# Spacing the weight, x and g tiles apart in SBUF, with one temporary slot fewer

## The chip, the cores and the metric

The kernel runs on one core of a Trainium2 chip. The metric is the device time of one execution in microseconds (us). Beside the timed executions there is one execution taken by the hardware profiler, and every view of the profile shown below is of that one.

## The reference

The program is an attention over a narrow band of scores, followed by a gated feed-forward layer, all in float32. Cut to what is computed:

```python
# q, k, v: (8 batches, 8 heads, 576, 64); tau = 0.02
scores = q @ k.T / sqrt(64)
scores = where(scores >= max(scores) - tau, scores, -1e9)   # row-wise maximum
attn = exp(scores - max(scores)); attn /= attn.sum() + 1e-9
x = (attn @ v)  # -> 4608 tokens x 512
gate = 1 / (1 + exp(-(x @ w_gate)))   # w_gate, w_val: 512 x 1536
val = x @ w_val
out = (gate * val) @ w_out            # w_out: 1536 x 512
```

## The kernel before, in words

**Numbers in two parts.** TensorE works in a single-pass float32 form (`F32R`), so an operand that has to be precise is split into a high part and a low part, and a product takes three matmuls (high·high, high·low, low·high). A tile with two parts is written as `[P, 2, 512]`: 4096 bytes in each of the 128 partitions.

**Two streams of work.** The attention goes through visits: one batch and one pair of heads, batch after batch. Each visit loads k, q and v, splits them, and goes through score tiles of 128 queries: scores `s` on TensorE (PE, L559), the maximum (DVE, L566), the threshold (L571 or L575), the exponential (ACT, L580), the masking with the row sums (DVE, L583), the normalisation (POOL, L613), transposes `tp` and `lk` (PE, L628, L657, L666) with their copies (L635, L638, L645, L672, L675), and the product with v, `av` (PE, L716 or L729), gathered in `xf` and split into an `x` tile (L738, L740). Batch 0 (`PLAIN`) uses plain float32 matmuls, four passes instead of the split.

The feed-forward part (called moe) goes through blocks of 512 tokens, eight from the batches and a ninth from the 64 left-over tokens of each batch. A block has `in_units`: for each of the 12 slices f of d_ff, 12 matmuls for the gate and 12 for the value, `m` (L781), then tanh into a temporary `th` (ACT, L791), the gated product (DVE, L795), and its split into a `g` tile (ACT L799, POOL L801). Then `out_units`: 4 output tiles of 36 matmuls each, `o` (L817), copied (ACT, L827) into a temporary `ot` and stored. Block 0 comes in two halves of 256 tokens. The weights are split once, in 36 conversions (L389 to L428, each with a temporary `wa`), written to DRAM and streamed back into `w` tiles for every later block (`wi` at L760 for m, `wo` for o).

**Tiles in memory.** All tiles of a tag rotate through a fixed number of slots (`SLOTS`): 7 of `w` (raw weights, split weights, streamed weights), 5 of `x`, 12 of `g` (and, early on, split weights `ws`), and 5 of `t2`, the 2048-byte temporaries: `wa` in a conversion, `th` from tanh to POOL's split, `avt` (L732) between two halves of `av`, and `ot`. Each w, x and g slot is 4096 bytes, so that all slots of these three tags begin at the same remainder of 512 bytes: in the built program it is 32 for each of them. The operands of one matmul start at multiples of 512 bytes within them. The operands of `s` and `av` start at multiples of 128 bytes within their tiles, which also begin at 32 past a multiple of 512 (or 288, for one of the `pl` slots). A tile `pad` of 224 bytes (`PAD = 56` floats) lies ahead of all.

**What sets the order.** The kernel issues nothing directly: every operation is recorded with its engine, an assumed cost and a key. `Plan.run` then goes through a list schedule with one free or busy flag for each engine; of the ready operations it takes the one with the smallest key whose tiles find room in `SLOTS`. moe matmuls have the lowest priority on PE (keys from 1e6), so they fill what the attention leaves. The order found this way is the program's order on each engine; on the chip each engine works through its own list and waits on semaphores. The number of `t2` slots thus counts twice: in the order, and on the chip, where a tile's next user waits for the last reader of the slot.

Of the kernel before, what the change touches and what calls it, by code (L numbers as in the profile page):

```python
# [2 lines left out]

# [39 lines left out]
class Plan:  # L43
# [12 lines left out]

    def make(self, b):
        pool, bufs = self.pools[b.tag]
        return pool.tile(b.shape, b.dtype, tag=b.tag, name=b.name, bufs=bufs)

    def op(self, eng, cost, key, emit, reads=(), writes=(), also=(), leave=0, behind=None, after=(), lag=0.0):

# [136 lines left out]
SLOTS = {  # L199
    "kn": 1, "qn": 1, "vn": 1, "k2": 1, "q2": 1, "kd": 3, "qd": 3, "vs": 2,  # L200
    "p": 3, "pc": 1, "sm": 8, "st": 8, "pt": 2, "pl": 2, "ptc": 1, "plc": 1, "xf": 2, "x": 5, "g": 12,
    "w": 7, "t2": 5,
}
PHASES = True
LEAD = 5
# [20 lines left out]
PE_UNTIL, POOL_UNTIL = 36, 72  # L226
AHEAD = 5

PAD = 56


def act(n):
# [16 lines left out]
def kernel(  # L249
# [48 lines left out]

    cp.tile([P, PAD], F32, tag="pad", name="pad")
    ident = cp.tile([P, P], F32, tag="ident", name="ident")  # L300
# [690 lines left out]
```

## Time and profile before

| | |
|---|---|
| median of 2 timed runs | 1477.87 us (1477.44 to 1478.29) |
| the profiled execution's own time | 1478.33 us |
| its span, first to last instruction | 1476.4 us |
| granted TensorE clock, mean | 0.986 |
| busy in the span: PE, DVE, ACT, POOL | 1428.2, 962.6, 792.5, 655.1 us |
| HBM traffic over the span | 172 GB/s |

The span leaves out 1.9 us of the profiled execution's time. PE is TensorE's matmuls and PEld its weight loads, one ahead of each matmul, which run beside the matmul before. A matmul's recorded duration (some 390 ns for 512 columns) is its latency; successive matmuls overlap, so that their pace is read from a group's time over its count in an undisturbed stretch. A row of the chain of waits gives the start, the length and the line of each piece of work that the end hung on, with the count of instructions in it. A row of the table by stretches gives each engine's busy time with its count in brackets, then the granted clock.

### The profile page before, as it was taken

Reading aid. Unit: us, or ns where it says so; the run is one execution under the profiler, and the core shown is the slowest. Engines: PE = TensorE matmul, PEld = TensorE weight load, DVE = VectorE, ACT = ScalarE, POOL = GpSimd, SP = SyncE. Lnnn points to the kernel's source line nnn. Section 1 sums busy time; section 2 is a strip of 40 time slices with the busy share of each in tenths; the row PEclk is TensorE's granted clock in tenths of the full one; section 3 lists DMA queues with packets and bytes.
Section 4 is the critical chain, followed back from the end, with each engine's and each line's share of the span. In section 5 each row is a group of like instructions: output and inputs, shape, how many; then the busy total and the mean of one; then the engine's idle time right before and its main releaser. Section 6 shows DMA issues by size and latency. Waiting matters only on the chain.

```text
span 1476.4 us, 23618 instructions
## 1 busy us (share of the span) xinstructions
PE 1428.2 (97%) x7960; PEld 1222.8 (83%) x7960; DVE 962.6 (65%) x2064; ACT 792.5 (54%) x1674; POOL 655.1 (44%) x766
## 2 busy tenths in 40 slices
PE   7899878899999999999999999999999999999998
PEld 4588778788888888888888888988888888888887
DVE  6888888888865897388918993789558852010010
ACT  6677656567645675376627663666456743121120
POOL 5668665654644355244533454444434442122120
PEclk9999979899999999999999999999999999999999
DMA  7877979686775658666666677557847454756663
GB/s 262 288 241 235 291 238 269 184 263 178 195 232 179 198 177 260 193 188 206 191 215 186 184 210 259 144 171 211 276 143 201 144 186 147 247 199 205 214 195 120
DMA packets 116551, 307.22 MB, mean 208 GB/s; under 512 B 17104, under 2 KB 38096, under 8 KB 116432
## 3 DMA queue, kind: packets, MB, share of 16 engines
q1 hardware_dynamic: 116432, 305.71, 67.1%
q8 instruction: 65, 1.06, 0.3%
q14 instruction: 54, 0.44, 0.1%
HBM read 224.92 MB, written 29.36 MB: 172 GB/s over the span
## 4 chain that ended last, share of the span: by engine, by line
PE 80%; DVE 8%; POOL 3%; ACT 3%; issue 2%; DMA 2%; SPq 0%; POOLq 0%; DVEq 0%; ACTq 0%
PE m L781 36%; PE o L817 17%; PE s L559 7%; PE av L729 7%; PE tp L628 5%; DVE p L583 2%; PE s_l L559 1%; DVE pt L645 1%; DVE st L566 1%; DVE sm L608 1%; POOL p L613 1%; DVE pl L675 1%; PE tp_l L628 1%; PE lk L666 1%; ACT p L580 1%
## 5 line engine op out<-in xcount | busy, mean ns | idle before, releaser
L781 PE MATMUL m<-x,wi 128*128 128x512 f32 x2016 | 495.7, 395 | 0.5 <-DMA wi<-wid 0.5
L781 PEld LDWEIGHTS m<-x,wi 128*128 128x128 f32 x2016 | 366.6, 188 | 69.2 <-issue 0.9
L817 PE MATMUL o<-g,wo 128*128 128x512 f32 x1296 | 343.7, 402 | 0.0
L613 POOL TENSOR_SCALAR p<-p,w_t,sm 128x576 f32<-128x576 f32 x224 | 188.2, 850 | 234.0 <-DVE sm L611 226.3
L795 DVE SCALAR_TENSOR_TENSOR th<-th,m 128x512 f32<-128x512 f32 (+1 forms) x120 | 75.8, 631 | 326.4 <-PE m L781 325.0
L801 POOL TENSOR_TENSOR g<-th,g 128x512 fp32r<-128x512 f32 (+1 forms) x120 | 141.6, 1180 | 307.7 <-ACT g L799 307.2
L817 PEld LDWEIGHTS o<-g,wo 128*128 128x128 f32 x1296 | 228.2, 189 | 37.9
L583 DVE SCALAR_TENSOR_TENSOR p<-s,st,p 128x576 f32<-128x576 f32 x224 | 181.2, 812 | 24.9 <-ACT p L580 17.8
L559 PE MATMUL s<-kd,qd 128*128 128x288 f32 x896 | 162.2, 305 | 13.1 <-DVE p L583 8.9
L580 ACT ACTIVATE p<-s,st 128x576 f32<-128x576 f32 x224 | 164.7, 737 | 13.3 <-DVE st L566 12.4
L799 ACT CAST g<-th 128x512 fp32r<-128x512 f32 (+1 forms) x120 | 69.1, 576 | 190.3 <-DVE th L795 190.3
L645 DVE TENSOR_TENSOR pt<-tp,pt 128x512 fp32r<-128x512 f32 x224 | 151.5, 687 | 25.4 <-ACT pt L638 19.2
L566 DVE TENSOR_REDUCE st<-s 128x1 f32<-128x576 f32 x224 | 163.4, 750 | 6.8 <-PE s L559 3.6
L559 PEld LDWEIGHTS s<-kd,qd 128*128 128x128 f32 x896 | 138.5, 191 | 35.4 <-DVE p L583 12.5
L638 ACT CAST pt<-tp 128x512 fp32r<-128x512 f32 x224 | 129.0, 587 | 49.1 <-PE tp L628 46.3
L729 PE MATMUL av<-pt,vs 128*128 128x320 f32 (+1 forms) x896 | 142.1, 302 | 1.0 <-DVE pt L645 0.6
L729 PEld LDWEIGHTS av<-pt,vs 128*128 128x128 f32 x896 | 133.7, 195 | 9.2 <-DVE pt L645 0.8
L628 PE MATMUL tp<-ident,p 128*128 128x128 f32 x896 | 131.8, 274 | 1.3 <-POOL p L613 1.0
L628 PEld LDWEIGHTS tp<-ident,p 128*128 128x128 f32 x896 | 108.3, 141 | 13.7 <-POOL p L613 4.5
L791 ACT ACTIVATE th<-m 128x512 f32<-128x512 f32 (+1 forms) x120 | 66.8, 556 | 96.4 <-POOL g L801 47.9
L571 ACT ACTIVATE st<-st,ntau_t 128x1 f32<-128x1 f32 x192 | 56.6, 295 | 92.3 <-DVE st L566 90.6
L733 DVE TENSOR_TENSOR xf<-av,avt 64x256 f32<-64x256 f32 x112 | 50.8, 454 | 37.3 <-ACT avt L732 36.1
(345 smaller groups left out, 1791.6 us busy)
## 6 DMA issues: line engine op xcount, KB each, us to landing
wi<-wid SPq DMA_DIRECT2D x192, 512.0 KB, 5.9
wo<-wod SPq DMA_DIRECT2D x108, 512.0 KB, 4.7
kd<-k SPq DMA_DIRECT2D x112, 320.0 KB, 5.3
qd<-q SPq DMA_DIRECT2D x112, 128.0 KB, 4.7
wid<-ws SPq DMA_DIRECT2D x24, 512.0 KB, 5.1
out_dram<-ot SPq DMA_DIRECT2D x36, 256.0 KB, 2.2
kn<-in_k_dram SPq DMA_DIRECT2D x28, 320.0 KB, 4.2
qn<-in_q_dram SPq DMA_DIRECT2D x28, 320.0 KB, 6.0
```

What stands on the lines that cost most here:

```text
L559: nc.tensor.matmul(s.ap[:, c, :HALF], st(), mv(slice(k0 + c * HALF, k0 + (c + 1) * HALF)), start=m == 0, stop=m == len(steps) - 1,)
L566: op("DVE", 0.76, key, lambda: nc.vector.tensor_reduce(out=st.ap[:, 0:1], in_=sv(), axis=AX.XY, op=ALU.max, negate=True), reads=[s], write ...
L580: op("ACT", 0.74, key, lambda: nc.scalar.activation(p(), sv(), AF.Exp, bias=st.ap[:, 0:1], scale=1.0), reads=[s, (st, 0)], writes=[(g.p, i)])
L583: op("DVE", 0.9, key, lambda: nc.vector.scalar_tensor_tensor(out=p(), in0=sv(), scalar=st.ap[:, 1:2], in1=p(), op0=ALU.is_ge, op1=ALU.mult ...
L613: op("POOL", 0.9, key, lambda i=i: nc.gpsimd.tensor_scalar(out=p.ap[:, i * S : (i + 1) * S], in0=p.ap[:, i * S : (i + 1) * S], scalar1=w_t ...
L628: nc.tensor.matmul(tp.ap[:, c, :], self.p.ap[:, o + c * P : o + (c + 1) * P], ident, is_transpose=True, start=c == 0, stop=c == NJ - 1, sk ...
L638: op("ACT", 0.58, key, lambda: nc.scalar.copy(hi(), tp.ap), reads=[tp], writes=[(self.pt, (0, i))])
L645: op("DVE", 0.69, key, lambda: nc.vector.tensor_tensor(out=lo(), in0=tp.ap, in1=f32(hi()), op=ALU.subtract), reads=[tp, (self.pt, (0, i))] ...
L729: nc.tensor.matmul(av.ap, st, mv, start=i == 0, stop=i == len(ms) - 1)
L781: nc.tensor.matmul(m.ap, wv[:, a, c * P : (c + 1) * P], xs[c].ap[:, z, c0:c1], start=e == 0, stop=e == 11,)
L801: op("POOL", pool(W), -1, lambda th=th, hi=hi, f=f: nc.gpsimd.tensor_tensor(out=g[f].ap[:, 1, c0:c1], in0=th.ap, in1=f32(hi()), op=ALU.sub ...
L817: nc.tensor.matmul(acc.ap, wv[:, f, a], g[fg * ND + f].ap[:, z], start=(fg, f, a, z) == (0, 0, 0, 0), stop=(fg, f, a, z) == (NFG - 1, ND - ...
```

## The change

Each w tile is allocated 8 floats longer than it is, each x and g tile 24 floats longer, and only the first part is used; the tile that the kernel sees has the shape and the contiguous layout that it had. The slots then lie 4128 bytes (w) and 4192 bytes (x, g) apart, so that in the built program the seven w slots begin at remainders of 512 of 384, 416, 448, 480, 0, 32 and 64, and the seventeen g and x slots take each multiple of 32 at least once. The room for this (1856 bytes) comes from `t2`, which has four slots instead of five, and from `PAD`. `PAD` also moves everything that lies ahead of the w tiles by 160 bytes: kd, qd and vs now begin at remainder 384, and the pt tiles, which lie behind them, at 96.

```diff
     def make(self, b):
         pool, bufs = self.pools[b.tag]
-        return pool.tile(b.shape, b.dtype, tag=b.tag, name=b.name, bufs=bufs)
+        if b.tag not in STAGGER:
+            return pool.tile(b.shape, b.dtype, tag=b.tag, name=b.name, bufs=bufs)
+        n = math.prod(b.shape[1:])
+        t = pool.tile([b.shape[0], n + STAGGER[b.tag]], b.dtype, tag=b.tag, name=b.name, bufs=bufs)
+        if len(b.shape) == 2:
+            return t[:, :n]
+        names = "abc"[: len(b.shape) - 1]
+        return t[:, :n].rearrange(
+            f"p ({' '.join(names)}) -> p {' '.join(names)}", **dict(zip(names[1:], b.shape[2:]))
+        )
...
     "p": 3, "pc": 1, "sm": 8, "st": 8, "pt": 2, "pl": 2, "ptc": 1, "plc": 1, "xf": 2, "x": 5, "g": 12,
-    "w": 7, "t2": 5,
+    "w": 7, "t2": 4,
 }
...
-PAD = 56
+PAD = 16
+
+STAGGER = {"w": 8, "g": 24, "x": 24}
```

No instruction is added or removed on any engine. The order changes, because the planner has one temporary slot fewer. On PE it differs from the second half of batch 0 (its first changed matmul ran at 88.8 us in the profiled execution) until shortly after batch 3's attention begins; everything behind that stands in the same order. In the new program the lines of these functions are 10 or 12 further down (L781 is L793, L559 is L571).

The first place is PE's list at the start of batch 1's attention (`s1_0_000`: the scores of batch 1, head pair 0, first tile). `m0_9_1_0` is the value part of slice 9 of block 0's first half, `av0_3b` the last product of batch 0. Before:

```order
L781 MATMUL m0_9_0_0_1672<-x0_3_764,ws9_0_1407 128x256 x3
L781 MATMUL m0_9_1_0_1707<-x0_0_339,ws9_1_1461 128x256 x3
L559 MATMUL s1_0_000_1715<-kd1_0_0_1067,qd1_0_0_1043 128x288 x4
L781 MATMUL m0_9_1_0_1707<-x0_1_465,ws9_1_1461 128x256 x3
L559 MATMUL s1_0_001_1726<-kd1_0_0_1067,qd1_0_0_1043 128x288 x4
L716 MATMUL av0_3b_02_1736<-pt0_3b_02_1666,vp0_3b_1249 64x256 x4
```

The same place with the change:

```order
L793 MATMUL m0_5_0_0_1429<-x0_1_465,ws5_0_832 128x256 x3
L793 MATMUL m0_5_0_0_1429<-x0_2_610,ws5_0_832 128x256 x3
L571 MATMUL s1_0_000_1462<-kd1_0_0_1055,qd1_0_0_1035 128x288 x4
L793 MATMUL m0_5_0_0_1429<-x0_3_764,ws5_0_832 128x256 x3
L728 MATMUL av0_3b_02_1475<-pt0_3b_02_1423,vp0_3b_1215 64x256 x4
L728 MATMUL av0_3b_02_1475<-pt0_3b_l4_1403,vp0_3b_1215 64x64 x4
```

Ahead of `s1_0_000` stood 231 moe matmuls of 256 columns, up to slice 9; now there are 117, up to slice 5. The other 114 have moved behind it. The attention's own matmuls ahead of this point are the same ones.

The second place is PE's list at the start of batch 3's attention, close to where the two orders become one again. `m1_6_1_0` is slice 6 of block 1. Before:

```order
L781 MATMUL m1_6_1_0_5188<-x1_1_3371,wi1_6_1_5014 128x512 x3
L781 MATMUL m1_6_1_0_5188<-x1_2_3378,wi1_6_1_5014 128x512 x3
L781 MATMUL m1_6_1_0_5188<-x1_3_3784,wi1_6_1_5014 128x512 x3
L559 MATMUL s3_0_000_5214<-kd3_0_0_4947,qd3_0_0_4942 128x288 x4
L781 MATMUL m1_7_0_0_5221<-x1_0_2443,wi1_7_0_5065 128x512 x2
```

With the change:

```order
L571 MATMUL s2_3_121_5153<-kd2_3_1_4605,qd2_3_1_4547 128x288 x4
L793 MATMUL m1_5_1_0_5145<-x1_0_2403,wi1_5_1_4929 128x512
L793 MATMUL m1_5_1_0_5145<-x1_1_3346,wi1_5_1_4929 128x512 x3
L571 MATMUL s3_0_000_5169<-kd3_0_0_4923,qd3_0_0_4904 128x288 x4
L793 MATMUL m1_5_1_0_5145<-x1_2_3353,wi1_5_1_4929 128x512 x3
```

Here 30 moe matmuls of 512 columns have moved behind `s3_0_000`: 2126 matmuls stood ahead of it, now 2096, and nothing else differs in what lies ahead of it on PE.

The third place is DVE's list at the start of batch 3's attention (`st3_0_000` is the maximum of the first score tile, `th1_6_0` the gated product of slice 6). Before:

```order
L795 SCALAR_TENSOR_TENSOR th1_6_0_5194<-th1_6_0_5194,m1_6_1_0_5188 128x512
L608 TENSOR_TENSOR sm2_3_12_5206<-sm2_3_12_5206,den_t_80 128x2
L611 RECIPROCAL sm2_3_12_5206<-sm2_3_12_5206 128x2
L566 TENSOR_REDUCE st3_0_000_5236<-s3_0_000_5214 128x1
L566 TENSOR_REDUCE st3_0_001_5243<-s3_0_001_5225 128x1
```

With the change:

```order
L595 SCALAR_TENSOR_TENSOR p2_3_12_5128,sm2_3_12_5159<-s2_3_120_5105,st2_3_120_5113,p2_3_12_5128 128x576
L578 TENSOR_REDUCE st2_3_121_5166<-s2_3_121_5153 128x1
L578 TENSOR_REDUCE st3_0_000_5177<-s3_0_000_5169 128x1
L595 SCALAR_TENSOR_TENSOR p2_3_12_5128,sm2_3_12_5159<-s2_3_121_5153,st2_3_121_5166,p2_3_12_5128 128x576
L807 SCALAR_TENSOR_TENSOR th1_5_0_5148<-th1_5_0_5148,m1_5_1_0_5145 128x512
```

Five DVE instructions have moved behind `st3_0_000`: two gated products (of slices 5 and 6), one masking of `p`, one addition and one reciprocal on `sm`. At batch 1's start it is more: 29 instructions, among them 7 conversions of three instructions each, 25 of the 36 conversions standing ahead of it before and 18 now.

More of the change, by code (lines that the diff above doesn't have):

```diff
@@ L1 @@
 import heapq
+import math
 from contextlib import ExitStack
```

## The prediction

> **What bounds the kernel now.** I read the totals of the page first, then a table by stretches of the span, then who made PE wait in each, then the chain of waits for the pace of the matmuls.
>
> ```profile
> span 1476.4 us, 23618 instructions
> PE 1428.2 (97%) x7960; PEld 1222.8 (83%) x7960; DVE 962.6 (65%) x2064; ACT 792.5 (54%) x1674; POOL 655.1 (44%) x766
> PE 80%; DVE 8%; POOL 3%; ACT 3%; issue 2%; DMA 2%; SPq 0%; POOLq 0%; DVEq 0%; ACTq 0%
> ```
>
> PE is busy for 97% of the span, but the average hides two regimes. The stretches separate them (us, then busy time of PE, PEld, DVE, ACT, POOL, each with its count, then the granted clock):
>
> ```profile
> 0.00:100.00 100.00, 84.04 (x429) 58.01 (x429) 79.81 (x163) 66.47 (x126) 63.88 (x94) 0.97 0.78 263
> 100.00:160.00 60.00, 59.58 (x419) 50.23 (x420) 47.85 (x94) 41.98 (x84) 47.58 (x62) 1.00 0.73 236
> 160.00:300.00 140.00, 115.63 (x753) 105.59 (x752) 121.64 (x260) 81.90 (x172) 87.71 (x127) 0.88 0.81 246
> 300.00:428.00 128.00, 127.02 (x752) 110.76 (x751) 111.37 (x254) 87.49 (x194) 62.76 (x69) 1.00 0.73 219
> 428.00:1190.00 762.00, 759.34 (x4337) 663.39 (x4336) 564.55 (x1232) 453.80 (x993) 336.59 (x369) 1.00 0.66 197
> 1190.00:1476.00 286.00, 282.61 (x1279) 234.76 (x1277) 37.43 (x65) 60.90 (x108) 56.60 (x48) 1.00 0.58 189
> ```
>
> From 300 us to the end PE never rests and runs at full clock. All that can be won or lost by order lies ahead of 300 us: 16.0 us of idle PE before 100, 0.4 from there to 160, 24.4 from 160 to 300, where the clock also falls to 0.88. What PE waited for, ahead of 300 and behind 440:
>
> ```profile
> PE s L559 <- DVE p L583: 6.8, 6, 2.2
> PE m L781 <- DVE wa L413: 3.2, 1, 3.2
> ...
> PE s L559 <- DVE p L583: 1.6, 5, 0.3
> PE m L781 <- DMA wi<-wid: 0.5, 1, 0.5
> ```
>
> The first two rows (160 to 300 us) name DVE: masking the scores and converting weights. The last two are all that this view lists for PE behind 440 us, 2.1 us together. There, only the pace of the matmuls counts, and the chain shows it (start, length, work, count):
>
> ```profile
> 858.28 1.07 PE av L729 x9
> 889.39 0.79 PE s_l L559 x6
> 890.18 34.48 PE m L781 x152
> 940.90 1.32 PE av L729 x9
> 950.50 1.38 PE o L817 x6
> 990.90 2.31 PE o L817 x10
> 1374.69 65.28 PE m L781 x288
> 1439.97 32.65 PE o L817 x144
> ```
>
> 65.28 us over 288 is 226.7 ns for 512 columns, as in the 32.65 us of 144. The two av rows are of 256 and 320 columns: 1.07 and 1.32 us over 9 are 119 and 147 ns. From 320 to 512 columns the pace grows by 80 ns, 0.417 ns per column; what is left is 226.7 - 213.3 = 13.3 ns for each matmul, whatever its length. That fixed part is the only thing that a tile's place could change.
>
> **The pace of the matmuls, first term.** The change moves where PE's two reads fall: the moving operand (x or g) and the weights (w) loaded beside it for the next matmul. Before, they differ by a multiple of 512 bytes; afterwards each multiple of 32 occurs. Does the 13.3 ns depend on that? Two rows speak. In s_l (0.79 us over 6: 132 ns for 288 columns, so 132 - 120 = 12 ns) the moving piece starts 256 or 1408 bytes on, at other multiples of 128 from the weights, and the fixed part is the same. And between the o matmuls of the interleaved stretch and the closing one, with the same offsets, 1.38 us over 6 and 2.31 over 10 are 230 and 231 ns against 226.7: there the state of the stream matters by 4 ns, places being equal. Steps of 32 to 96 bytes are in no row. I bound the term from both sides: at best the fixed part vanishes. The matmuls concerned are m and o:
>
> ```profile
> L781 PE MATMUL m<-x,wi 128*128 128x512 f32 x2016 | 495.7, 395 | 0.5 <-DMA wi<-wid 0.5
> L817 PE MATMUL o<-g,wo 128*128 128x512 f32 x1296 | 343.7, 402 | 0.0
> L781 PE MATMUL m<-xl,wi 128*128 128x512 f32 x288 | 65.4, 389 | 0.0
> ```
>
> 2016 + 1296 + 288 = 3600 of 512 columns, and 576 of 256 in block 0: 4176 by 13.3 ns is 55.6 us. At worst it doubles, the same sum upwards. Nearest to the rows (s_l, and the 4 ns of the stream's state) lies no change; I take 0. The av matmuls get a new offset as well (1008 by 13.3 ns, 13.4 us at either end) and are taken at 0 with the same argument.
>
> The Trainium skill says the same in SBUF — State Buffer, section "Who interferes with whom": PE has two SBUF read ports, one for the moving operand and an independent one for weight loads, and never waits on anyone; by that the term is 0. The trace agrees in that ACT, POOL and DMA work beside the 288 matmuls of 65.28 us leaves them at 226.7 ns each. But its TensorE: Matmul & The Clock Gate, section "Wait — 56ns, not 53.3ns?", gives columns over 2.4 GHz and about 2.5 ns for warm matmuls back to back, an estimate of 215.8 ns for 512; the trace has 10.9 ns more, which speaks for something that better places might remove: 4176 by 10.9 ns, 45.5 us, if all of it went.
>
> **The order, second term.** With four t2 slots the planner postpones 114 moe matmuls of 256 columns behind batch 1's first scores, which ran at 146.2 us:
>
> ```profile
> L559 PE MATMUL s<-kd,qd x896: 288/295/607, 146.2 to 1196.1; 128*128 128x288 f32 x180
> ...
> 0.00:422.49 422.49, 380.76 (x2318) 319.78 (x2319) 357.15 (x760) 274.88 (x567) 259.03 (x347) 0.95 0.78 243
> ```
>
> 114 by 119 ns is 13.6 us of PE work. It leaves a stretch where PE had no room (0.4 us idle in 60) and lands where PE had 24.4 us idle. If the attention, which has lost 7 conversions on DVE ahead of it, moves up into the gap, nothing is lost and part of the later holes is filled. If it can't, 13.6 us are lost and won back only as far as the holes take them. DVE had 60 - 47.85 = 12.2 us free from 100 to 160, so at best the attention gains 12 us; at worst the order costs 13.6.
>
> Between these, the point where the orders meet again decides. The first scores of batch 3 (at 422.49 us; the second row counts the matmuls ahead of it) now have 30 moe matmuls of 512 columns fewer ahead of them: 30 by 226.7 ns is 6.8 us that PE still owes when the attention gets there. What paces the attention up to 300 us is DVE, which has five instructions fewer to do by then:
>
> ```profile
> L795 DVE SCALAR_TENSOR_TENSOR th<-th,m 128x512 f32<-128x512 f32 x96 | 65.8, 685 | 321.9 <-PE m L781 321.5
> L583 DVE SCALAR_TENSOR_TENSOR p<-s,st,p 128x576 f32<-128x576 f32 x224 | 181.2, 812 | 24.9 <-ACT p L580 17.8
> L608 DVE TENSOR_TENSOR sm<-sm,den_t 128x2 f32<-128x2 f32 x112 | 39.4, 351 | 3.1
> L611 DVE RECIPROCAL sm<-sm 128x2 f32<-128x2 f32 x112 | 18.5, 165 | 3.7
> ```
>
> 2 by 0.685, 0.812, 0.351 and 0.165 are 2.7 us. If DVE stays as full as it was, the attention is there 2.7 us earlier, and PE, never resting from then on, ends 6.8 - 2.7 = 4.1 us later. I take +4.1, between -12.2 and +13.6.
>
> **The slot on the chip, third term.** Behind 440 us the order is the old one, and a temporary's reuse comes one turn earlier. In the closing stretch a slice takes 24 matmuls, 5.44 us, and a th lives from tanh to POOL's split:
>
> ```profile
> 1301.33 0.60 ACT L791 ACTIVATE th<-m 128x512 f32<-128x512 f32 x1 [1.37 <-PE m L781]
> ...
> 1305.55 1.29 POOL L801 TENSOR_TENSOR g<-th,g 128x512 fp32r<-128x512 f32 x1 [3.88 <-ACT g L799]
> ```
>
> From 1301.33 to 1306.84 are 5.5 us; four slots last 21.8 us. In the mixed stretches avt takes slots between, but ACT and POOL are busy 60% and 44% there, and nothing on PE waits for them. Cost 0, hidden by these spare turns; without that cover each late th would hold a PSUM bank and PE with it, which only the early stretch could show.
>
> **Sum.** The profiled execution took 1478.33 us, 1.9 more than its span: 1478.3 + 0 + 4.1 + 0 = 1482.4, and the median shown stands 0.5 below it, so 1482 us against 1477.87.
>
> **The rivals.** *Places cost.* Where weights and moving operand now fall badly, reads hold each other up and the fixed part doubles at half of the offsets: 4176 by 13.3 by one half, 27.8 us, 1510 us. It passes 2% from 6 ns a matmul (29.6 - 4.1 us over 4176). For it: the stream's state already moves the pace by 4 ns, and x changes its offset every third matmul. Against: the equal fixed part in s_l. *Places pay.* Half of the offsets lose the fixed part: 1454 us; all, 1426. For it: 13.3 ns that no column accounts for; against, the same row. TensorE: Matmul & The Clock Gate of the Trainium skill, as weighed above, stands on this rival's side. *The order costs.* PE starves from 100 to 146 and the holes don't take the work: 1478 + 13.6 = 1492. For it: conversions hold their t2 slot while they wait for a g slot, so tanh finds none. *The order pays.* The attention moves up by DVE's free 12.2 us and the postponed matmuls fill the holes: 1466. For it: DVE's 86% from 160 to 300. That the change does nothing to places is excluded by the slot sizes, 4128 and 4192 bytes.
>
> **How the numbers follow.** The forecast has 0.56, with 1470 to 1492 for itself; places cost 0.13, places pay 0.11, the order costs 0.10 and pays 0.10. The range reaches to the middle of both place cases: 1452 to 1510. A measurement of this kernel tells about 2%, 29.6 us, from no change. Faster by that: most of places pay, 0.07. Slower: most of places cost with a tail of the order, 0.11. Within: 0.82.
>
> **What would show it.** Right: 288 matmuls in 65.3 us in the closing blocks, waits of PE behind 440 us of some 2 us, and PE's idle time ahead of 300 us spread differently, some 4 us more up to batch 3. Wrong: long runs whose pace differs between x tiles or w tiles, or a mean off 226.7 ns (each ns is 3.6 us); PE waiting for tanh or for the split (L803, L813) ahead of 300 us; or new waits behind 440.

## The result, and the profile after

The changed kernel takes 1496.19 us (median of 2 runs, 1494.54 to 1497.84) against 1477.87: a ratio of 1.0117, 95% interval 1.0084 to 1.015. It is slower by some 18 us, less than the 2% that counts as a change but clearly more than nothing, though there are only two timed runs on each side. The profiled execution took 1494.54 us, its span is 1492.7, 16.3 longer than before.

The totals of the page:

```profile
span 1492.7 us, 23655 instructions
PE 1438.5 (96%) x7960; PEld 1222.2 (82%) x7960; DVE 962.5 (64%) x2064; ACT 790.7 (53%) x1674; POOL 652.6 (44%) x766
```

The instructions on each working engine are the same in number, and the busy time of DVE, ACT and POOL is the same within 3 us. PE's has grown by 10.3 us with the same 7960 matmuls. The stretches show where (columns as in the prediction):

```profile
0.00:100.00 100.00, 84.36 (x427) 57.74 (x428) 78.44 (x160) 65.66 (x125) 63.27 (x94) 0.97 0.76 258
100.00:160.00 60.00, 58.88 (x417) 49.53 (x414) 42.45 (x91) 39.84 (x81) 42.20 (x58) 1.00 0.62 187
160.00:300.00 140.00, 112.11 (x753) 104.03 (x754) 125.50 (x266) 83.36 (x173) 91.61 (x130) 0.88 0.84 265
300.00:428.00 128.00, 124.57 (x736) 108.62 (x737) 113.56 (x258) 87.69 (x196) 61.47 (x69) 1.00 0.77 221
428.00:1190.00 762.00, 759.65 (x4302) 659.25 (x4301) 555.68 (x1207) 447.63 (x980) 332.33 (x363) 1.00 0.65 195
```

Up to 428 us idle PE time has gone from 41.7 us to 48.1: 1.1 instead of 0.4 from 100 to 160, 27.9 instead of 24.4 from 160 to 300, and 3.4 instead of 1.0 behind 300. From 428 to 1190 PE is as full as before (759.65 us against 759.34), at full clock, but has done 4302 matmuls instead of 4337 (a part of that because the stretch begins some 5 us further back in the program). That is a loss that no wait shows. Its waits behind 440 us are as few as before, 2.3 us against 2.1:

```profile
PE s L571 <- DVE p L595: 1.6, 5, 0.4
PE s L571 <- DVE p_l L595: 0.7, 4, 0.2
```

The end of the chain of waits gives the pace, in the same pieces of work as before (start, length, work, count):

```profile
1056.26 35.27 PE m L793 x152
1206.23 41.82 PE m L793 x180
...
1288.27 66.96 PE m L793 x288
1355.22 33.37 PE o L829 x144
1388.60 66.92 PE m L793 x288
1455.52 33.41 PE o L829 x144
```

66.96 us over 288 is 232.5 ns, where it was 226.7; 35.27 over 152 is 232.0, where 34.48 gave 226.8. In the interleaved stretch, however, the same view has

```profile
1106.44 1.40 PE o L829 x6
1157.95 2.32 PE o L829 x10
```

233 and 232 ns, where the prediction quoted 230 and 231 of before. The long undisturbed runs have lost their pace; the short ones had less of it to lose.

To part the two terms I take the point where both programs have issued the same matmuls again, the start of the 2357th (the first of slice 8 of block 1). The row of before, then that of after; the count in PE's bracket is that of the matmuls ahead of it:

```profile
0.00:429.87 429.87, 388.14 (x2356) 326.14 (x2357) 362.46 (x774) 279.25 (x576) 262.75 (x351) 0.95 0.77 240
```

```profile
0.00:434.72 434.72, 386.63 (x2356) 325.33 (x2357) 364.63 (x778) 279.01 (x577) 264.34 (x354) 0.95 0.76 236
```

4.9 us of the 16.3 are lost by there, 11.4 behind it.

### The profile page after: what moved, and what is told of

Its sections match the earlier page's. It is cut to its first block, busy times and chain, and to the rows that moved or that the text cites. A ratio compares the mean times of both kernels' runs of the same rounds, so it can differ in the third digit from the quotient of the medians.

```text
span 1492.7 us, 23655 instructions
## 1 busy us (share of the span) xinstructions
PE 1438.5 (96%) x7960; PEld 1222.2 (82%) x7960; DVE 962.5 (64%) x2064; ACT 790.7 (53%) x1674; POOL 652.6 (44%) x766
## 4 chain that ended last, share of the span: by engine, by line
PE 82%; DVE 10%; ACT 3%; issue 2%; DMA 2%; POOL 1%; SPq 0%; DVEq 0%; ACTq 0%; POOLq 0%
PE m L793 38%; PE o L829 17%; PE s L571 7%; PE av L741 7%; PE tp L640 5%; DVE p L595 2%; PE s_l L571 1%; DVE pt L657 1%; DVE sm L620 1%; DVE st L578 1%; DVE wb L422 1%; DVE pl L687 1%; DVE wb L418 1%; ACT p L592 1%; PE lk L678 1%
## 5 line engine op out<-in xcount | busy, mean ns | idle before, releaser
L793 PE MATMUL m<-x,wi 128*128 128x512 f32 x2016 | 502.6, 399 | 0.0
L793 PEld LDWEIGHTS m<-x,wi 128*128 128x128 f32 x2016 | 367.4, 188 | 75.9
L829 PE MATMUL o<-g,wo 128*128 128x512 f32 x1296 | 347.3, 405 | 0.0
L625 POOL TENSOR_SCALAR p<-p,w_t,sm 128x576 f32<-128x576 f32 x224 | 185.2, 836 | 237.1 <-DVE sm L623 227.5
L571 PE MATMUL s<-kd,qd 128*128 128x288 f32 x896 | 162.8, 306 | 19.9 <-DVE p L595 14.6
L571 PEld LDWEIGHTS s<-kd,qd 128*128 128x128 f32 x896 | 139.7, 193 | 42.3 <-DVE p L595 15.6
```

The costliest lines, as they stand in the source:

```text
L571: nc.tensor.matmul(s.ap[:, c, :HALF], st(), mv(slice(k0 + c * HALF, k0 + (c + 1) * HALF)), start=m == 0, stop=m == len(steps) - 1,)
L625: op("POOL", 0.9, key, lambda i=i: nc.gpsimd.tensor_scalar(out=p.ap[:, i * S : (i + 1) * S], in0=p.ap[:, i * S : (i + 1) * S], scalar1=w_t ...
L793: nc.tensor.matmul(m.ap, wv[:, a, c * P : (c + 1) * P], xs[c].ap[:, z, c0:c1], start=e == 0, stop=e == 11,)
L829: nc.tensor.matmul(acc.ap, wv[:, f, a], g[fg * ND + f].ap[:, z], start=(fg, f, a, z) == (0, 0, 0, 0), stop=(fg, f, a, z) == (NFG - 1, ND - ...
```

## The experiments

The theory after the result: two independent causes, the order with four temporaries (some 5 us, ahead of 430 us) and the pace of matmuls whose two reads lie at other offsets (some 11 us, behind it). Rivals: that the order, or the reuse of four slots on the chip, is the whole; and, for the pace, that it is not the offset itself that costs but its change from tile to tile, which never lets the stream settle.

### The two parts by themselves

The first kernel keeps the four temporaries and `PAD = 16`, without the spacing; the second keeps the spacing, with five temporaries.

```diff
-STAGGER = {"w": 8, "g": 24, "x": 24}
+STAGGER = {}
```

> The change without the spacing: four temporaries and PAD 16, tiles back to back. If the split into two terms is right, this keeps the new order's 4 to 5 us at batch 3 and the old pace of 226.7 ns in the closing blocks: 1482 to 1484 us. If the spacing is all that costs: 1478. If four temporaries cost more on the chip behind 440 us: over 1486.

```diff
-    "w": 7, "t2": 4,
+    "w": 7, "t2": 5,
```

> The spacing with five temporaries (the old order, PAD 16): if the spacing costs through the pace alone, the closing blocks run at 232 ns a matmul and the total is 10 to 13 us over before, 1488 to 1491. If the cost is the order's alone: 1478.

Measured side by side with the kernel before (1479.17 us there): the order alone 1481.6 us, ratio 1.0015 (1.0001 to 1.0029); the spacing alone 1489.98 us, ratio 1.007 (1.0048 to 1.0093). The closing rows of the chain, order alone and spacing alone:

```profile
1281.67 65.28 PE m L793 x288
1346.95 32.64 PE o L829 x144
```

```profile
1283.50 66.96 PE m L793 x288
1350.45 33.48 PE o L829 x144
```

and the 2357th matmul, in the same order:

```profile
0.00:435.37 435.37, 385.86 (x2356) 323.89 (x2357) 363.28 (x778) 279.31 (x577) 264.39 (x354) 0.96 0.76 236
```

```profile
0.00:429.78 429.78, 385.07 (x2356) 321.88 (x2357) 362.09 (x774) 278.63 (x576) 262.26 (x351) 0.96 0.76 240
```

The order alone has the old pace to the hundredth of a microsecond, and is 5.5 us late at the 2357th matmul; the spacing alone is 0.1 us early there and has the new pace. In spans (1481.3 and 1488.2 against 1476.4) the parts are 4.9 and 11.8 us, 16.7 together against 16.3 with both. These are single executions, and the timed ones of the kernel before alone went from 1475.55 to 1483.15 us, so the sum agrees better than it had to. The two pieces of the span are steadier than the whole: in the four traces with the old order (before, the spacing alone, and the two kernels with other places further below) the 2357th matmul starts at 429.0 to 430.5 us, in the two with the new order at 434.7 and 435.4; from there to the start of the last matmul it is 1041.9 to 1042.7 us in the three traces whose offsets are all multiples of 256 bytes, and 1054.2 to 1057.2 in the three where they are not. The timed ratios multiply to 1.0085, at the lower end of the interval of the change. The spacing alone came out as expected, the order alone 0.4 us under the expected 1482 to 1484; that four slots cost something on the chip behind 440 us is excluded by the first, which ends no later than it was at the 2357th matmul.

### The pace by itself, at chosen offsets

A kernel that computes nothing of the reference: two large tiles, and 22 groups of 120 matmuls of the kernel's form, with weights and moving operand at chosen places. In each group the 12 matmuls of a unit go through the same places as in the kernel; only the spacing differs. In a row, the first function shifts the moving operand and the second the weights, in floats of 4 bytes; then come the weight columns and the moving columns.

```diff
+    ("qa", kernel_pattern(same(0), same(0)), 128, 512),
+    ("qd", kernel_pattern(same(0), same(24)), 128, 512),
+    ("qg", kernel_pattern(step(24), same(0)), 128, 512),
+    ("qk", kernel_pattern(step(128), same(0)), 128, 512),
+    ("ql", kernel_pattern(lambda c, i: 24 * ((i // 12) % 2), same(0)), 128, 512),
+    ("qn", kernel_pattern(same(8), same(8)), 128, 512),
...
```

> Leaves out the whole computation: 22 groups of 120 split-float32 matmuls each (128x512, weights and moving operand read at chosen places of two large tiles), to measure the pace by itself. Theory A (the stream of matmuls and weight loads settles when the offset between its two reads stays the same, and is thrown out when it changes): groups with one constant offset (qa 0, qb 32, qc 64, qd 96, qe 16, qf 8 bytes, qn both moved by 32) all at 226 to 228 ns; groups whose offset changes at every third matmul (qg by 96, qi as in the changed kernel) at 231 to 234; qh (w alone, every third) the same; ql (every twelfth) between, 228 to 230; qp (once in 120) at 227. Theory B (some offsets are bad in themselves): the constant offsets of 32 and 96 bytes cost 4 ns or more, and ql lies at the mean of qa and qd. If the fixed 13 ns come from the weight load, fewer weight columns (qr 64, qs 32) shorten it.

The groups by cost (busy time of 120 after the bar, us; offset 0 stands in qw, at the end, since qa waited for its data):

```profile
L97 PE MATMUL qd<-xb,wb 128*128 128x512 f32 x120 | 28.3, 396 | 0.0
L97 PE MATMUL qe<-xb,wb 128*128 128x512 f32 x120 | 28.2, 396 | 0.0
L97 PE MATMUL qb<-xb,wb 128*128 128x512 f32 x120 | 28.2, 395 | 0.0
L97 PE MATMUL qg<-xb,wb 128*128 128x512 f32 x120 | 28.0, 394 | 0.0
L97 PE MATMUL qi<-xb,wb 128*128 128x512 f32 x120 | 28.0, 394 | 0.0
L97 PE MATMUL ql<-xb,wb 128*128 128x512 f32 x120 | 28.0, 394 | 0.0
L97 PE MATMUL qs<-xb,wb 128*32 128x512 f32 x120 | 28.0, 394 | 0.0
L97 PE MATMUL qf<-xb,wb 128*128 128x512 f32 x120 | 27.8, 393 | 0.0
L97 PE MATMUL qk<-xb,wb 128*128 128x512 f32 x120 | 27.4, 389 | 0.0
L97 PE MATMUL qn<-xb,wb 128*128 128x512 f32 x120 | 27.4, 389 | 0.0
L97 PE MATMUL qw<-xb,wb 128*128 128x512 f32 x120 | 27.4, 389 | 0.0
```

Theory A falls: constant offsets of 16, 32 and 96 bytes (qe, qb, qd) cost no less than changing ones (qg), 0.8 to 0.9 us over 120 matmuls, 7 ns each; even 8 bytes (qf, 27.8 us) cost 3 to 4. What reaches the old pace is offset 0 (qw), both operands moved by 32 bytes together (qn), and x tiles 512 bytes apart (qk). From start to start, leaving out the first dozen of each group, the pace is 226.7 ns in these, 233.4 for 32 and 234.3 for 96 bytes, 232.5 with both spacings of the change (qi), as in its closing blocks. Theory B isn't whole either: ql, which changes between 0 and 96 bytes every twelfth matmul, is at 232.4, not at the mean of 230.5, because its dozens at offset 0 take 229.8 ns a matmul and those at 96 bytes 234.6: behind a bad offset, eight matmuls of each dozen at the good one go by before the pace settles; qp, which changes once in 120, lies at the mean, 230.5. And the 13 ns aren't the length of the weight load: with 32 weight columns (qs) instead of 128 the pace is 231.7.

### Which offsets are good

The same kernel with one constant offset to a group, 16 of them at 512 columns and five at each of three other lengths.

```diff
+    ("aw", kernel_pattern(same(0), same(48)), 128, 512),
+    ("ay", kernel_pattern(same(0), same(64)), 128, 512),
...
```

> Leaves out the whole computation: 31 groups of 120 matmuls, each at one constant offset between moving operand and weights; 16 offsets of 0 to 480 bytes at 512 columns, then 0, 32, 128, 256 and 384 bytes at 256, 320 and 288 columns. If only a multiple of 512 bytes is good at 512 columns: aq 226.7 ns, all fifteen others 229 to 236. If 128 or 256 bytes are good as well, au, ay and bs lie at 226.7. If some offset removes the fixed part, one group lies below 224. At 256 columns offset 0 stays at 120 ns and 32 bytes at 118 to 119, so that the sign turns with the length.

```profile
L106 PE MATMUL ar<-xb,wb 128*128 128x512 f32 x120 | 28.2, 395 | 0.0
L106 PE MATMUL at<-xb,wb 128*128 128x512 f32 x120 | 28.3, 396 | 0.0
L106 PE MATMUL aw<-xb,wb 128*128 128x512 f32 x120 | 27.6, 391 | 0.0
L106 PE MATMUL ay<-xb,wb 128*128 128x512 f32 x120 | 27.4, 389 | 0.0
L106 PE MATMUL bu<-xb,wb 128*128 128x512 f32 x120 | 27.6, 391 | 0.0
L106 PE MATMUL cr<-xb,wb 128*128 128x320 f32 x120 | 17.8, 309 | 0.0
L106 PE MATMUL cs<-xb,wb 128*128 128x320 f32 x120 | 17.8, 309 | 0.0
L106 PE MATMUL cx<-xb,wb 128*128 128x288 f32 x120 | 16.2, 295 | 0.0
L106 PE MATMUL cz<-xb,wb 128*128 128x288 f32 x120 | 16.0, 294 | 0.0
L106 PE MATMUL bw<-xb,wb 128*128 128x256 f32 x120 | 14.6, 283 | 0.0
L106 PE MATMUL bx<-xb,wb 128*128 128x256 f32 x120 | 14.4, 281 | 0.0
```

From start to start, in ns for one matmul of 512 columns (place of the weights minus place of the moving operand, in bytes; 256 more gives the same to 0.1 ns):

```
offset   0 (256)  32 (288)  64 (320)  96 (352)  128 (384)  160 (416)  192 (448)  224 (480)
pace     226.7    233.4     233.4     234.3     232.5      233.3      228.9      233.3
```

The period is 256 bytes, half of what was expected, and 0 is the best of it: no group is below 226.7, so that the fixed 13.3 ns can't be placed away by any offset tried. The gain that half of the offsets were to bring in one rival exists at none of them. The mean of the eight is 232.0 ns; the changed kernel, whose m and o matmuls take all eight about equally often in the built program, runs at 232.5 in its closing blocks. The sign does turn with the length: at 256 columns the offsets 0 and 256 take 120.0 ns and the others 118.3 to 118.7; at 320 all five take 146.7; at 288 it is 131.7 against 133.4.

### One constant offset in the whole kernel, and 512 bytes between x tiles

Both from the kernel before, with its own order, five temporaries and `PAD = 56`. In the first, the tile that lies just ahead of the g and x tiles (`q2`) is 32 bytes longer, so that all g and x tiles begin 32 bytes later and the w tiles stay; in the second, each x slot is 512 bytes longer.

```diff
+STAGGER = {"q2": 8}
```

> The kernel before with one spacing alone: g and x tiles lie 32 bytes further on, all of them, so that every streamed weight has the one offset of 32 bytes from what it multiplies and nothing changes from tile to tile; five temporaries, the old order. If an offset costs by its size: 233.4 ns in the closing blocks, 6.7 ns over 3600 matmuls, 24 us, 1500 to 1504. If changes of the offset cost and a constant one doesn't: 226.7 ns and 1478.

```diff
+STAGGER = {"x": 128}
```

> The kernel before with x tiles 512 bytes apart from each other: the spacing differs between x tiles, but every offset stays a multiple of 512. If only the remainder of 512 counts: 226.7 ns in the closing blocks and 1476 to 1481 us, no change. If unequal tiles cost as such: the m matmuls at 230 ns or more and the total 6 us or more over before.

Measured (before 1478.04 us beside them): 1491.7 us, ratio 1.0086 (1.0057 to 1.0116), and 1476.78 us, ratio 0.9989 (0.9972 to 1.0005). The closing rows of the two:

```profile
1286.14 67.20 PE m L793 x288
1353.34 33.60 PE o L829 x144
```

```profile
1275.13 65.28 PE m L793 x288
1340.41 32.64 PE o L829 x144
```

With one single offset (the moving operand 32 bytes further on, 224 in the table) a matmul takes 233.3 ns, as in the group, without any change from tile to tile, and x slots that are 512 bytes further apart cost nothing: it is the remainder that counts, in the kernel as in the groups. The expected total of the first was nearly twice too large. I had charged 6.7 ns to 3600 matmuls, but only those that had settled could lose all of it. Counted over the trace of before by their place in an unbroken run of m and o matmuls (leaving out the ones whose gap holds the end of another kind), the first four take 231.2 to 232.1 ns on average, the fifth to eleventh 227.6 to 229.8, and 1893 from the twelfth on 226.7. 1893 by 6.6 ns is 12.5 us, against 13.7 timed; the matmuls in the second to eleventh place lose less, 230.3 ns before and 232.4 here on average. With the change's own 5.8 ns it is 11.0 us, against 11.4 behind the 2357th matmul.

### Fewer breaks in the runs

If a run needs a dozen matmuls to settle, a planner that breaks in less often should win some of the rest. Two kernels on the base of before, in which moe matmuls are recorded in steps of 4 and 6 instead of 2:

```diff
-        step = 2 if W == SM else 3
+        step = 4 if W == SM else 3
...
-                for j in range(0, 12, 2):
+                for j in range(0, 12, 4):
```

> The kernel before, tiles where they were, but the planner may break into the moe matmuls only after each 4 instead of each 2 (whole blocks): 391 runs of moe matmuls instead of 472. If moe matmuls cost more just behind another kind of matmul (230 to 236 ns in the first seven or so against 226.7), fewer breaks save up to 2 to 4 us: 1474 to 1477, unless the attention waits longer for PE. If the breaks cost nothing: 1478, or more by the order's share.

> As the run with 4, with breaks only after each 6: 344 runs, most of 6 or 12. Up to 3 to 6 us saved if the start of a run costs, 1472 to 1476; over 1480 if scores and transposes that wait behind 1.4 us of moe matmuls starve the attention.

With 4: 1477.41 us against 1477.65, ratio 0.9994 (0.998 to 1.0008), no difference; from 3.0 us faster to 1.2 slower, the interval leaves room for part of the 2 to 4 us that fewer breaks were to save. With 6: 1482.22, ratio 1.0029 (1.0014 to 1.0044), slower. PE, which rested for 2.7 us from 428 to 1190 us, now rests for 5.5, and it waits for DVE's masking:

```profile
428.00:1190.00 762.00, 756.49 (x4305) 660.31 (x4303) 557.83 (x1209) 447.29 (x981) 334.96 (x366) 1.00 0.66 197
```

```profile
PE s_l L571 <- DVE p L595: 2.6, 5, 0.5
PE s L571 <- DVE p_l L595: 2.3, 5, 0.5
```

That a longer step makes the attention late fits these rows but wasn't tested by itself; what the pace may have gained isn't to be seen. No kernel of this study is measurably faster than the one before the change.

## Why the prediction was right or wrong, by its own steps

- **What bounds the kernel**: right. Behind 440 us the waits of PE that the profile lists are 2.3 us together, and the whole loss there is in the pace.
- **First term, the pace, 0**: this step failed. It cost 11.4 us behind the 2357th matmul, of which 5.8 ns for each of the 1893 settled matmuls make 11.0. That the forecast's range holds the time all the same is luck as far as this term goes. Two readings led to it. The row of s_l was the wrong witness: its 288 columns lie at a length where the offset makes 1.7 ns, and av's 320 at one where it makes none; neither says anything on 512. One of the two offsets of s_l, 256 bytes, is a good one besides. And the 226.7 ns of the long runs were taken as the rule and the 230 and 231 of the interleaved ones as a disturbance. They showed that a well placed matmul of this length can lose most of what a bad place costs (230 to 232 against 232.5 to 234.3 ns), so that the good pace is the special case. The prediction had the clue in its own quoted rows. The av matmuls, also taken at 0, lost nothing: those of 320 columns show no offset, and those of 256 columns went from 118.9 to 118.0 ns, under 1 us over all of them.
- **The Trainium skill's rule** in SBUF — State Buffer, "Who interferes with whom", that PE's two reads are independent and PE waits for no one, by which the first term would be 0 too, isn't borne out for these two reads: their distance modulo 256 bytes moves the pace by up to 7.6 ns (226.7 to 234.3). The 215.8 ns of TensorE: Matmul & The Clock Gate of the Trainium skill, section "Wait — 56ns, not 53.3ns?", an estimate from its formula for 512 columns, is reached at no offset.
- **Second term, the order, +4.1**: right in size, and the trace follows the mechanism given; that DVE's five missing instructions are what brought the attention there earlier was not tested by itself. Batch 1's first scores came at 131.4 us instead of 146.2 (the attention did move up into the gap), and the first scores of batch 3 at 420.2, 2.3 us early where 2.7 were worked out from DVE's five missing instructions. The 30 matmuls owed, 6.8 us less the 2.3, then made it 4.9 us late in the profile of the change, 5.5 in that of the order alone; timed, the order's share is 0.0015 of 1479 us, 2.2 us, interval 0.1 to 4.3.

```profile
L571 PE MATMUL s<-kd,qd x896: 288/295/606, 131.4 to 1205.9; 128*128 128x288 f32 x180
...
0.00:420.18 420.18, 372.09 (x2288) 313.21 (x2288) 353.71 (x758) 271.74 (x563) 254.61 (x345) 0.95 0.77 240
```

- **Third term, the slot, 0**: right behind 440 us. The order alone is 4.9 us late in its span, and was 5.5 late at the 2357th matmul. Ahead of 440 us the slot's share on the chip isn't parted from the order's: ACT waits there for POOL's split to free a conversion's temporary, 3.0 us in both traces with four slots against 0.7 before, and no run shows whether that reaches PE.
- **The rivals**: *places cost* had the sign and the place, and its witness, that the stream's state already moved the pace, pointed the right way; its size, 13.3 ns at half of 4176 matmuls, was two and a half times too large. It happened together with the forecast's order term, as the rival had it too (1510 is 1482 + 27.8): 1482 + 11 is 1493, against 1496.2 measured. *Places pay* is refuted at every offset tried with 512 columns.
- **The range**, 1452 to 1510, holds the time. The likeliest case's own range, 1470 to 1492, does not: the time is inside because the range was drawn to the middle of a rival that had 0.13, and the forecast of 1482 foresaw 4 of the 18 us.

What stays open: why 256 bytes, why lengths differ in sign, and what makes a run settle at once in some groups and late in others. The runs show a pace by offset and length, not the memory's inside.

## What to carry to other kernels

Look at where the two operands of a matmul begin relative to each other: for long runs of single-pass float32 matmuls of 512 columns, keep moving operand and weights at a distance of a multiple of 256 bytes, and check what paddings and freed temporaries elsewhere do to that remainder. A change that leaves an engine as busy as before and adds no wait can still cost: compare the count of instructions done in the same stretch, or the length of one long piece of the chain. And take a witness of the same shape: a matmul of another length says nothing on this one.

## What the runs showed of the hardware that was not expected

- The pace of 512-column single-pass float32 matmuls depends on the distance from the moving operand to the weights modulo 256 bytes, at the multiples of 32 tried: 226.7 ns at 0, 228.9 at 192, 232.5 to 234.3 elsewhere; at 256 columns 0 is the slower one, 120.0 against 118.3 to 118.7.
- In the kernel the good pace takes about a dozen matmuls to set in after another kind: 231 to 232 ns for the first four, 226.7 from the twelfth on. In the groups it took 3 to 10, and none in two of them (ql and ay).
- The pace doesn't follow the weight load: 32 weight columns instead of 128 make a load of 109 ns instead of 188, and matmuls of 231.7 ns instead of 226.7.

```profile
L97 PEld LDWEIGHTS qs<-xb,wb 128*32 128x32 f32 x120 | 13.1, 109 | 14.7
L97 PEld LDWEIGHTS qw<-xb,wb 128*128 128x128 f32 x120 | 22.5, 188 | 4.7
```
